# In the h stage of a chain of experts: a22 a product later, a step's sums ahead of the right sides, four later loads

## The chip, the cores and the metric

The kernel runs on one core of one Trainium2 chip. The metric is the device time of one execution, in microseconds (us). Below, PE is TensorE (its matmuls; PEld is its weight loads), DVE is VectorE, ACT is ScalarE, POOL is GpSimd, and SP is SyncE, which here only issues DMAs. SPq and ACTq are the sequencers of SP and ACT at issuing a DMA.

## The reference

The program computes an attention with 32 packed keys, a gated product of experts and a second pair of layers; the last part is what the change touches.

```python
x = attention(q, k, v, p)                 # 4608 tokens, 512 features
x = ((x @ w1) * (x @ w2)) @ w3 @ w_out    # w3 @ w_out is made first
h = x @ w_in                              # 512 -> 2048
g = where(h >= 1, h, where(h <= -1, 0, (h + 1)**2 / 4))
out = g @ w_out                           # 2048 -> 512
```

## The kernel before

Both products of the second pair of layers are made by a scheme of seven products of quarter matrices in place of eight (A11, S1, S2, A12, S4, S3, A22 are the names of the products). Every factor is kept as a high and a low part in fp32r, and a product takes three passes (high by high, high by low, low by high) over two halves of its inner dimension: six matmuls of 128x128 weights by N columns.

**The h stage** (lines 980 to 1020) has 40 steps. A step makes one 128-row piece of each quarter of h for one group of tokens; PAIRS lists five groups, each of two halves of 512 tokens (the last of 256, so N = 256 there). `divmod(s, 8)` gives the group t and the place i in it. In step s PE runs product(s, A11), product(s, S1), then product(s - 1, A22) of the step before, then S2, A12, S4 and S3 of step s. Four products of a step share one PSUM bank, "x": A11 begins it, S2, S3 and A22 add to it, and between them its value is read out. ACT copies it after A11 (m1) and after S2 (u2), and S1's bank after S1 (m5). DVE makes the sums by `add` (line 877): the first upper half from A12's bank and m1, the second from S4's bank and u2, and the first lower half from bank x after S3 and m5. A22 adds to the same bank x, so it can't begin before this last sum has read it. These sums are called the first, second and third sum of a step.

The step after applies the function g: `upper` (relu and square on ACT, two minima on DVE by line 816, a store), `upper_end` (a difference on DVE, line 843, and a store), `lower_begin`, `lower_relu`, `lower_middle` (relus and a square on ACT, two minima on DVE; the second relu and minimum read bank x after A22) and `lower_end` (a 1024-wide difference on DVE, line 866, and a store of 1 MB). The buffers U, L and r exist twice. The store DMAs are collected and issued by SP at the end of the step in program order (`flush_stores`); each waits for its data on SP, and what is behind it in SP's order waits too.

The left sides (weights of w_in, high and low) stay in memory as tiles of 1 MB: n = 0 for i = 0 to 3 and n = 1 for i = 4 to 7. All ten loads are issued by SP ahead of step 0 (lines 766 to 775). Those of S4 and A22 are streamed instead: `ws_load(s + 1)` is issued by ACT behind product(s - 1, A22), into two buffers.

The right sides of the next group (x2s tiles, high and low) are made within the steps by `x2_tasks`: a list of eleven tasks, in order parts(A11), a combination, a combination, parts(S1), a combination, parts(S2), parts(A12), parts(S4), parts(S3), a combination, parts(A22). A part is an ACT copy (line 672) and a DVE subtraction (line 673), a combination a DVE subtraction (line 667), all 1024 wide. `tasks(n)` runs the next n: MID says how many run behind the first sum of a step i, LAST how many at its end; step i = 0 has one more right behind m1's copy. The group's load (`x2_load`, 2 MB) is issued at the start of step i = 1.

**The output stage** (lines 1069 to 1093) has 140 pieces x = (group, product, quarter j) of 12 matmuls. SP loads a piece of g (`g_load`, line 930, 512 KB; two for a piece of A22, which `g_combine` on line 939 subtracts on DVE); `g_parts` makes its high part on ACT (line 947) and low part on DVE (line 948), three pieces ahead (AHEAD). In the last group of h, `first_sides` (line 957) already loads the output stage's first left sides (`w2_load`, line 907) and first pieces of g.

Of the kernel before, what the change touches and what calls it, by code (L numbers as in the profile page):

```python
# [30 lines left out]
PAIRS = [(0, 512), (1024, 512), (2048, 512), (3072, 512), (4096, 256)]  # L31

A11, S1, S2, A12, S4, S3, A22 = range(7)
# [22 lines left out]
def fused_kernel(ctx: ExitStack, tc, qT, kT, vv, pb, w1, w2, w3T, wo, win, wout, out):  # L56
# [673 lines left out]
    def buf(tag):  # L730
        if tag in first:
            return first.pop(tag)
        shape, bufs = KINDS[tag]
        return hp.tile(shape, F32, name=tag, tag=tag, bufs=bufs)
# [6 lines left out]
    def wi_load(i, n):  # L741
        nc.sync.dma_start(out=wi_t[i, n].bitcast(F32), in_=wid[i][n])
# [4 lines left out]
    def ws_load(s, eng):  # L747
        if s < 8 * len(PAIRS):
            t = ws_t[s] = first.pop("ws", None) or ws_tile()
            eng.dma_start(out=t.bitcast(F32), in_=wst[s % 8 // 4][:, s % 4])  # L750
# [20 lines left out]
    for i in (S2, A12, S3):  # L771
        wi_load(i, 0)
    ws_load(1, nc.sync)
    for i in (A11, S1, S2, A12, S3):
        wi_load(i, 1)


    BANK = {A11: "x", S1: "z", A12: "y", S2: "x", S4: "z", S3: "x", A22: "x"}
# [4 lines left out]
    def psb(b):  # L783
        return first.pop(b) if b in first else psB.tile([P, 512], F32, name=b, tag=b, bufs=BUFS[b])

    bank = {}

    def product(s, q):
        t, i = divmod(s, 8)
        N = PAIRS[t][1]  # L790
        b = BANK[q]
        if q in (A11, S1, A12):
            bank[s, b] = psb(b)
        n, c0 = divmod(i, 4)
        j = 0
        for k in range(2):
            for v, m in PASSES:
                if q in STREAM:
                    w = ws_t[s][:, STREAM.index(q), k, v, :]
                else:  # L800
                    w = wi_t[q, n][:, k, v, c0 * P:(c0 + 1) * P]
                nc.tensor.matmul(  # L802
                    bank[s, b][:, :N], w, x2_t[t, q][:, m, k, :N],
                    start=(j == 0 and q in (A11, S1, A12)), stop=(j == 5), skip_group_check=True,
                )
                j += 1
# [14 lines left out]
    def flush_stores():  # L821
        while stores:
            stores.pop(0)()

    def store(s, a, n, x):
        t, i = divmod(s, 8)
        stores.append(lambda: nc.sync.dma_start(out=gd[t][:, a:a + n, i], in_=x))
# [12 lines left out]
    def upper_end(s):  # L840
        N = PAIRS[s // 8][1]
        h = kept[s, 0]
        nc.vector.tensor_tensor(out=h[:, 2, :N], in0=h[:, 1, :N], in1=h[:, 0, :N], op=ALU.subtract)
        store(s, GT1, 1, h[:, 2:3, :N])

    def lower_begin(s):
        N = PAIRS[s // 8][1]
        r = kept[s, "r"] = buf("r")[:, :, :N]
        relu(r[:, 1], kept[s, 1][:, 1, :N])
# [21 lines left out]
    def copy(tag, ps, N):  # L871
        c = buf(tag)[:, :N]
        nc.scalar.activation(out=c, in_=ps[:, :N], func=AF.Copy)  # L873
        return c
# [7 lines left out]
    def tasks(n):  # L882
        for _ in range(n):
            if todo:
                todo.pop(0)()
# [11 lines left out]
    def half_tile(pool, tag):  # L897
        return pool.tile([P, 2, 2, 512], F32R, name=f"h{tag}", tag=tag, bufs=1).rearrange(
            "p a b (c n) -> p (a b c) n", c=2).rearrange("p (k v) n -> p k v n", v=2)

    def w2_tile(q, pool, tag):
        w = pool.tile([P, 4, 1024], F32R, name=f"w2{q}", tag=tag, bufs=1)
        w2_t[q] = [w[:, 2 * x:2 * x + 2].rearrange("p a (b n) -> p (a b) n", n=256).rearrange(
            "p (k v) n -> p k v n", v=2) for x in range(2)]

    def w2_load(q, x, k, n):
        nc.sync.dma_start(out=w2_t[q][x][:, k:k + n].bitcast(F32), in_=w2d[q][:, 4 * x + k:4 * x + k + n])
# [7 lines left out]
    def raw_tile(n):  # L915
        return buf("r") if n > 3 else ring("raw", n, [P, 2, 512], F32)
# [4 lines left out]
    def g_load(most=len(seq)):  # L921
        while count[0] < most:
            t, q, j = seq[count[0]]
            N = PAIRS[t][1]
            parts = (G21, GT2) if q == A22 else (PART[q],)
            if count[2] + len(parts) > RAWS:
                return
            for a in parts:
                g = raw_tile(count[1] % RAWS)
                nc.sync.dma_start(out=g[:, :, :N], in_=gd[t][:, a, 2 * j:2 * j + 2])  # L930
                rawg.setdefault(count[0], []).append(g[:, :, :N])
                count[1] += 1
                count[2] += 1
            count[0] += 1

    def g_combine(x):
        if x < len(seq) and seq[x][1] == A22:
            a, b = rawg[x]
            nc.vector.tensor_tensor(out=a, in0=a, in1=b, op=ALU.subtract)
# [10 lines left out]

    MID = {2: 2, 3: 1, 4: 1, 5: 1, 7: 1, 0: 2}
    LAST = {7: 2}


    def first_sides(s):
        i = s - (steps - 8)
        if i == 1:
            w2_tile(A11, late["f"], "f")  # L960
        if i in (1, 2, 3):
            w2_load(A11, (i - 1) // 2, 2 * (i - 1) % 4, 2)
        if i in (4, 5):
            w2_load(A11, 1, i - 2, 1)
        if i == 4:
            wq.release()
            late["raw"] = tc.alloc_tile_pool(name="rw", bufs=1, side="right", reuse_waits="tile")
            for n in range(4):
                tiles["raw", n] = raw_tile(n)
            w2_t[S1] = [half_tile(hp, f"wi{A11}0"), None]  # L970
        if i >= 4:
            g_load(i - 3)
        if i == 6:
            w2_load(S1, 0, 0, 2)
        if i == 7:
            w2_load(S1, 0, 2, 2)
            w2_t[S1][1] = half_tile(hp, f"wi{A11}1")
            w2_load(S1, 1, 0, 4)

    for s in range(steps):  # L980
        t, i = divmod(s, 8)
        N = PAIRS[t][1]
        if i == 1 and t + 1 < len(PAIRS):
            x2_load(t + 1)
            todo = x2_tasks(t + 1)
        product(s, A11)
        m1 = copy("m1", bank[s, "x"], N)
        if i == 0:
            tasks(1)
        if s:  # L990
            upper(s - 1)
            if i:
                upper_end(s - 1)
            lower_begin(s - 1)
        product(s, S1)
        m5 = copy("m5", bank[s, "z"], N)
        if s:
            product(s - 1, A22)
            ws_load(s + 1, nc.scalar)
        product(s, S2)  # L1000
        if s:
            lower_relu(s - 1)
        u2 = copy("u2", bank[s, "x"], N)
        if s:
            lower_middle(s - 1)
        product(s, A12)
        kept[s, 0] = buf("U")
        add(kept[s, 0][:, 0, :N], bank.pop((s, "y")), m1, N)
        if s and i:
            lower_end(s - 1)  # L1010
        tasks(MID.get(i, 0))
        kept[s, 1] = buf("L")
        product(s, S4)
        add(kept[s, 0][:, 1, :N], bank.pop((s, "z")), u2, N)
        product(s, S3)
        add(kept[s, 1][:, 1, :N], bank[s, "x"], m5, N)
        if s and i == 0:
            upper_end(s - 1)
            lower_end(s - 1)
        tasks(LAST.get(i, 0))  # L1020
        flush_stores()
        first_sides(s)
    product(steps - 1, A22)
    late["b1"].release()
# [10 lines left out]
    lower_end(steps - 1)  # L1035
    flush_stores()
    g_load()
    w2_t[S2] = [half_tile(wp, f"wi{i}0") for i in (S1, S2)]
    w2_t[A12] = [half_tile(wp, f"wi{i}1") for i in (S1, S2)]
    w2_t[S3] = [half_tile(wp, f"wi{A12}1"), half_tile(wo2, f"wi{S3}1")]  # L1040
# [3 lines left out]
    AHEAD = 3  # L1044
# [25 lines left out]
    for x, (t, q, j) in enumerate(seq):  # L1070
        N = PAIRS[t][1]
        b = BANK[q]
        start = j == 0 and q in (A11, S1, A12)
        if start:
            bank[b] = [psb(b) for _ in range(2)]
        for d in range(2):
            for k in range(2):
                for n, (s, v) in enumerate(PASSES):
                    nc.tensor.matmul(  # L1079
                        bank[b][d][:, :N], w2_t[q][j // 2][:, 2 * (j % 2) + k, s, d * P:(d + 1) * P], op[x][:, k, v, :N],  # L1080
                        start=start and k == 0 and n == 0, stop=(j == 3 and k == 1 and n == 2), skip_group_check=True,
                    )
        if x:
            flush_stores()
        if j == 3:
            evacuate(t, q, bank[b])
        if x == 0:
            g_parts(2)
        g_parts(x + AHEAD)
        g_load()  # L1090
        if t == 0 and q in order[:5]:
            w2_load(order[order.index(q) + 2], j // 2, 2 * (j % 2), 2)
        g_combine(x + AHEAD + 2)
    flush_stores()
    psB.release()
    dl.release()
# [60 lines left out]
```

## Time and profile before

| | |
|---|---|
| median of 3 runs | 1381.49 us (1380.85 to 1383.59) |
| profiled execution, its own time | 1377.88 us |
| its span | 1376.2 us |
| busy in the span: PE, PEld, DVE, ACT | 1286.0, 1066.3, 879.9, 672.1 us |
| h stage, first product to first matmul of the output stage | 617.26 to 1010.13 us |
| matmuls of the h stage (line 802), of the output stage (line 1079) | 1680, 1680 |

Times inside the trace are microseconds from the span's start. A row of the timeline gives start and duration, engine, line, operation, out<-in by the program's names, shapes and count, and in brackets how long the engine stood idle before it and what ended that. PE's busy time is not its peak, since ends of matmuls are modelled. A wait is put down to the one that came last by the profile.

### The profile page before, as it was taken

The numbers are of one execution on the slowest core, as the hardware profiler recorded it, in microseconds if no ns is written. First come the engines' busy times: TensorE is split into PE (matmuls) and PEld (weight loads), VectorE is DVE, ScalarE is ACT, GpSimd is POOL, SyncE is SP. The second block draws the span as 40 slices with busy tenths as digits, with TensorE's granted clock in tenths as the row PEclk, the third lists the DMA queues.
The fourth block names the chain that finished last, engine by engine and source line by source line (L and its number), as shares of the span: only waits on it lengthen the run. The fifth ranks groups of instructions, "written<-read, shape, count | busy, mean of one in ns | idle before, by whom it ended". The sixth has DMA issues, their size and how long they took to land.

```text
span 1376.2 us, 21142 instructions
## 1 busy us (share of the span) xinstructions
PE 1286.0 (93%) x8184; PEld 1066.3 (77%) x8184; DVE 879.9 (64%) x1462; ACT 672.1 (49%) x1144; POOL 0.7 (0%) x6
## 2 busy tenths in 40 slices
PE   6798799999999999998999989999889799999998
PEld 2365678888898989996777777778768688888888
DVE  4694387687686779534676777776664445555454
ACT  3353254545454545434576656656554243434433
POOL 0000000000000000000000000000000000000000
PEclk9899999999999999999899999999999999999999
DMA  8763366565575543359548575576899877768675
GB/s 277 240 204 112 117 225 189 187 218 179 187 243 171 209 175 134 129 177 364 186 165 298 203 257 194 176 254 223 266 385 372 317 263 234 255 229 284 221 224 173
DMA packets 124916, 306.78 MB, mean 223 GB/s; under 512 B 10384, under 2 KB 45200, under 8 KB 121360
## 3 DMA queue, kind: packets, MB, share of 16 engines
q1 hardware_dynamic: 87920, 236.09, 49.4%
q10 hardware_dynamic: 36896, 69.35, 14.9%
q8 instruction: 64, 1.05, 0.3%
q14 instruction: 36, 0.29, 0.1%
HBM read 199.36 MB, written 106.04 MB: 222 GB/s over the span
## 4 chain that ended last, share of the span: by engine, by line
PE 60%; DVE 15%; DMA 10%; ACT 9%; issue 5%; ACTq 1%; SPq 1%; DVEq 0%
PE x L1079 13%; PE psk L402 12%; PE psk L378 11%; PE z L1079 6%; PE x L802 6%; PE y L1079 4%; ACT r L810 3%; DMA g<-U 3%; PE z L802 2%; PE psk L486 2%; ACT r L813 2%; PE psk L194 2%; DMA raw<-w3T 1%; DVE L L866 1%; DVE U L877 1%
## 5 line engine op out<-in xcount | busy, mean ns | idle before, releaser
L402 PEld LDWEIGHTS psk<-g,w 128*128 128x128 f32 x1500 | 200.2, 188 | 26.3 <-ACT st L429 15.7
L378 PE MATMUL psk<-at,m 128*128 128x288 f32 x1494 | 215.2, 300 | 3.9 <-DVE at L329 1.9
L378 PEld LDWEIGHTS psk<-at,m 128*128 128x128 f32 x1494 | 202.2, 189 | 18.0 <-issue 8.6
L402 PE MATMUL psk<-g,w 128*128 128x288 f32 x1500 | 209.1, 297 | 2.6 <-ACT st L429 1.3
L802 PE MATMUL x<-x2s,wi 128*128 128x512 f32 (+1 forms) x720 | 165.9, 375 | 0.0
L802 PEld LDWEIGHTS x<-x2s,wi 128*128 128x128 f32 x720 | 129.1, 192 | 24.7
L948 DVE TENSOR_TENSOR op<-raw,op 128x1024 fp32r<-128x1024 f32 (+1 forms) x94 | 101.2, 1111 | 63.8 <-ACT op L947 63.8
L947 ACT ACTIVATE op<-raw 128x1024 fp32r<-128x1024 f32 (+1 forms) x94 | 87.1, 968 | 83.3 <-DVE L L1056 34.3
L1079 PE MATMUL x<-op,w 128*128 128x512 f32 (+1 forms) x480 | 102.7, 373 | 8.0 <-DVE op L948 8.0
L1079 PEld LDWEIGHTS x<-op,w 128*128 128x128 f32 x480 | 84.9, 191 | 25.0 <-DVE op L948 9.7
L1079 PE MATMUL x<-op,hwi 128*128 128x512 f32 (+1 forms) x480 | 100.4, 368 | 0.0
L1079 PEld LDWEIGHTS x<-op,hwi 128*128 128x128 f32 x480 | 83.1, 188 | 15.8
L802 PE MATMUL x<-x2s,ws 128*128 128x512 f32 (+1 forms) x240 | 61.0, 390 | 29.3 <-DVE L L877 29.0
L816 DVE SCALAR_TENSOR_TENSOR U<-U,r 128x512 f32<-128x512 f32 (+1 forms) x80 | 47.4, 634 | 54.5 <-ACT r L813 54.5
L390 DVE TENSOR_TENSOR tb<-psk,ta 128x288 f32<-128x288 f32 x124 | 56.1, 452 | 37.6 <-ACT ta L388 19.2
L813 ACT ACTIVATE r<-r 128x1024 f32<-128x1024 f32 (+1 forms) x80 | 78.1, 976 | 1.3
L948 DVE TENSOR_TENSOR op<-r,op 128x1024 fp32r<-128x1024 f32 (+1 forms) x46 | 50.0, 1115 | 44.4 <-ACT op L947 44.3
L486 PE MATMUL psk<-wo,w3f 128*128 128x512 f32 x128 | 64.7, 659 | 14.4 <-DVE w3f L135 14.4
L802 PEld LDWEIGHTS x<-x2s,ws 128*128 128x128 f32 x240 | 41.2, 192 | 46.3 <-DVE L L877 29.4
L873 ACT ACTIVATE m<-x 128x512 f32<-128x512 f32 (+1 forms) x40 | 22.2, 554 | 106.5 <-PE x L802 103.7
L124 ACT ACTIVATE cvt<-raw 128x512 f32<-128x512 f32 x72 | 48.3, 675 | 48.5 <-DMA raw<-w 22.7
L388 ACT ACTIVATE ta<-psk 128x288 f32<-128x288 f32 x125 | 50.4, 403 | 28.5 <-PE psk L378 24.2
(111 smaller groups left out, 1901.9 us busy)
## 6 DMA issues: line engine op xcount, KB each, us to landing
raw<-g SPq DMA_DIRECT2D x86, 512.0 KB, 4.9
g<-L SPq DMA_DIRECT2D x32, 1024.0 KB, 4.1
r<-g SPq DMA_DIRECT2D x42, 512.0 KB, 5.5
ws<-ws ACTq DMA_DIRECT2D x38, 512.0 KB, 4.5
g<-U SPq DMA_DIRECT2D x64, 256.0 KB, 4.2
w<-hl ACTq DMA_DIRECT2D x28, 512.0 KB, 3.4
x2d<-st ACTq DMA_DIRECT2D x72, 144.0 KB, 3.5
wi<-hl ACTq DMA_DIRECT2D x20, 512.0 KB, 5.4
```

Of the source, the lines that this page charges most:

```text
L124: nc.scalar.activation(out=t, in_=raw.bitcast(F32).rearrange("p (n two) -> p n two", two=2)[:, :, 1], func=AF.Copy, scale=2.0 ** -112)
L378: nc.tensor.matmul(ps[w][:, :HS], m_tile[b, w, n][:, s, G, c0 * P:(c0 + 1) * P], at_tile[b][:, G, v, hf * HS:(hf + 1) * HS], start=(k == 0 ...
L388: nc.scalar.activation(out=bs, in_=ps[1][:, :HS], func=AF.Copy)
L390: nc.vector.tensor_tensor(out=g, in0=ps[0][:, :HS], in1=bs, op=ALU.mult)
L402: nc.tensor.matmul(ps, w34[kt][:, s, mt * P:(mt + 1) * P], g_t[kt, hf][:, v, :], start=(kt == kts[0] and n == 0), stop=(kt == kts[-1] and ...
L486: nc.tensor.matmul(acc[4 * hf + m], w3f[hf, j][:, m * P:(m + 1) * P], wof[j], start=(j == 0), stop=(j == 7))
L802: nc.tensor.matmul(bank[s, b][:, :N], w, x2_t[t, q][:, m, k, :N], start=(j == 0 and q in (A11, S1, A12)), stop=(j == 5), skip_group_check= ...
L813: nc.scalar.activation(out=r, in_=r, func=AF.Square)
L816: nc.vector.scalar_tensor_tensor(out=out, in0=h, scalar=1.0, in1=r, op0=ALU.max, op1=ALU.min)
L947: nc.scalar.activation(out=o[:, :, 0, :N], in_=a[0], func=AF.Copy)
L948: nc.vector.tensor_tensor(out=o[:, :, 1, :N], in0=a[0], in1=o[:, :, 0, :N].bitcast(F32), op=ALU.subtract)
L1079: nc.tensor.matmul(bank[b][d][:, :N], w2_t[q][j // 2][:, 2 * (j % 2) + k, s, d * P:(d + 1) * P], op[x][:, k, v, :N], start=start and k == ...
```

## The change

In a step, product(s, S2) and its copy u2 now come ahead of product(s - 1, A22). The tasks that ran behind the first sum of steps i = 2 to 5 run at the end of the step, as does `lower_end` (but for i > 0 of the last group); i = 0 has one behind the first sum (parts(S3), so far right behind m1's copy) and two at the end, i = 7 stays as it was with one and two. The loads of the second halves of left sides (n = 1) are issued by SP at the end of steps 0 to 3, behind the stores of the step. One 1 MB load of the output stage's S1 moves from the end of the last step to behind the final stores and the loads of the next pieces of g. `g_combine` runs one piece later, next to that piece's `g_parts`.

```diff
     ws_load(1, nc.sync)
-    for i in (A11, S1, S2, A12, S3):
-        wi_load(i, 1)
...
-    MID = {2: 2, 3: 1, 4: 1, 5: 1, 7: 1, 0: 2}
-    LAST = {7: 2}
+    MID = {7: 1, 0: 1}
+    LAST = {2: 2, 3: 1, 4: 1, 5: 1, 7: 2, 0: 2}
...
             w2_t[S1][1] = half_tile(hp, f"wi{A11}1")
-            w2_load(S1, 1, 0, 4)
...
         m1 = copy("m1", bank[s, "x"], N)
-        if i == 0:
-            tasks(1)
...
         m5 = copy("m5", bank[s, "z"], N)
+        product(s, S2)
+        u2 = copy("u2", bank[s, "x"], N)
         if s:
             product(s - 1, A22)
             ws_load(s + 1, nc.scalar)
-        product(s, S2)
-        if s:
             lower_relu(s - 1)
-        u2 = copy("u2", bank[s, "x"], N)
-        if s:
             lower_middle(s - 1)
         product(s, A12)
         kept[s, 0] = buf("U")
         add(kept[s, 0][:, 0, :N], bank.pop((s, "y")), m1, N)
-        if s and i:
+        short = t + 1 == len(PAIRS) and i
+        if short:
             lower_end(s - 1)
         tasks(MID.get(i, 0))
...
         add(kept[s, 1][:, 1, :N], bank[s, "x"], m5, N)
-        if s and i == 0:
-            upper_end(s - 1)
+        tasks(LAST.get(i, 0))
+        if s and not short:
+            if i == 0:
+                upper_end(s - 1)
             lower_end(s - 1)
-        tasks(LAST.get(i, 0))
         flush_stores()
+        for w in {0: (A11,), 1: (S1,), 2: (S2, A12), 3: (S3,)}.get(s, ()):
+            wi_load(w, 1)
         first_sides(s)
...
     g_load()
+    w2_load(S1, 1, 0, 4)
...
-        g_combine(x + AHEAD + 2)
+        g_combine(x + AHEAD + 1)
```

## Rows read from the trace of the kernel before

**Rows 1.** The page: its first line, and a DMA issue (KB each, us to landing).
```profile
span 1376.2 us, 21142 instructions
...
g<-L SPq DMA_DIRECT2D x32, 1024.0 KB, 4.1
```
**Rows 2.** Who waited for whom, PE, the h stage.
```profile
PE x L802 <- DVE L L877: 29.0, 24, 7.1
```
**Rows 3.** Stretches cut at starts of steps: length, busy us (count), PEclk, DMA share, GB/s.
```profile
644.76:664.67 19.91, 12.76 (x43) 9.90 (x42) 10.11 (x13) 7.18 (x9) 0.00 (x0) 0.74 0.65 232
664.67:704.29 39.62, 39.05 (x169) 31.32 (x168) 27.65 (x40) 26.59 (x36) 0.00 (x0) 1.00 0.62 212
704.29:736.35 32.06, 29.66 (x127) 23.43 (x126) 25.23 (x34) 21.23 (x28) 0.00 (x0) 1.00 0.64 234
736.35:788.26 51.91, 49.19 (x211) 39.13 (x210) 37.08 (x52) 32.63 (x44) 0.00 (x0) 1.00 0.64 221
778.65:788.26 9.61, 9.61 (x43) 7.89 (x42) 6.16 (x10) 8.01 (x11) 0.00 (x0) 1.00 0.66 219
788.26:821.53 33.27, 30.97 (x128) 24.65 (x126) 25.38 (x34) 21.11 (x28) 0.00 (x0) 0.95 0.66 235
821.53:873.15 51.62, 49.20 (x212) 39.12 (x210) 36.80 (x51) 32.63 (x44) 0.00 (x0) 1.00 0.63 215
873.15:906.41 33.26, 30.97 (x128) 24.63 (x126) 25.33 (x34) 20.68 (x28) 0.00 (x0) 0.95 0.64 220
906.41:955.39 48.98, 48.46 (x211) 39.13 (x210) 34.13 (x51) 31.22 (x44) 0.00 (x0) 1.00 0.63 216
955.39:979.40 24.01, 17.65 (x127) 16.82 (x126) 16.57 (x33) 13.55 (x26) 0.00 (x0) 0.93 0.70 225
979.40:1010.13 30.73, 27.14 (x218) 25.83 (x217) 20.34 (x50) 19.68 (x43) 0.00 (x0) 1.00 1.00 328
```
**Rows 4.** Timeline of steps 15 to 17 (they start at 778.65, 788.26, 798.48).
```profile
786.09 0.69 DVE L816 SCALAR_TENSOR_TENSOR L<-x,r 128x512 f32<-128x512 f32 x1 [1.09 <-ACT r L813]
...
787.90 1.22 DVE L866 TENSOR_TENSOR L<-L,U 128x1024 f32<-128x1024 f32 x1
789.03 1.22 DVE L673 TENSOR_TENSOR x2s<-f,x2s 128x1024 fp32r<-128x1024 f32 x1
...
799.71 1.06 ACT L672 ACTIVATE x2s<-f 128x1024 fp32r<-128x1024 f32 x1 [3.09 <-DVE f L667]
...
800.67 0.58 ACT L873 ACTIVATE m<-x 128x512 f32<-128x512 f32 x1
...
803.37 2.03 PE L802 MATMUL x<-x2s,ws 128*128 128x512 f32 x6 [1.98 <-DVE L L877]
```
**Rows 5.** Timeline of steps 0 to 3, and a stretch there as in rows 3.
```profile
623.58 2.62 SPq L742 DMA_DIRECT2D wi<-wi  x5
...
649.35 0.69 DVE L877 TENSOR_TENSOR U<-y,m 128x512 f32<-128x512 f32 x1 [5.47 <-DMA g<-U]
...
637.00:647.00 10.00, 10.00 (x45) 8.23 (x44) 3.47 (x6) 5.53 (x8) 0.00 (x0) 1.00 1.01 409
```
**Rows 6.** Timeline of the last group, step 34.
```profile
975.29 0.42 DVE L877 TENSOR_TENSOR L<-x,m 128x256 f32<-128x256 f32 x1 [3.61 <-DMA g<-L]
```
**Rows 7.** Timeline of the output stage's start.
```profile
1022.69 1.06 ACT L947 ACTIVATE op<-r 128x1024 fp32r<-128x1024 f32 x1 [6.17 <-DMA r<-g]
...
1023.80 0.50 PE L1079 MATMUL z<-op,hwi 128*128 128x512 f32 x1 [2.40 <-ACT op L947]
...
1025.06 9.22 PE L1079 MATMUL z<-op,hwi 128*128 128x512 f32 x32 [0.76 <-DVE op L948]
```
**Rows 8.** Timeline of the output stage's first A22.
```profile
1077.32 1.06 ACT L947 ACTIVATE op<-raw 128x1024 fp32r<-128x1024 f32 x1 [4.31 <-DVE raw L939]
...
1084.90 1.22 DVE L939 TENSOR_TENSOR raw<-raw,raw 128x1024 f32<-128x1024 f32 x1 [6.55 <-DMA raw<-g]
...
1087.31 4.78 PE L1079 MATMUL x<-op,w 128*128 128x512 f32 x12 [5.52 <-DVE op L948]
```

## The prediction

> **What bounds the kernel now.** All the edits lie in two stages, so I read those and leave attention and the first expert layers aside. The profiled execution took 1377.88 us around a span of 1376.2 us [rows 1]; the median of the runs shown is 1381.49, 3.6 us above it. I make the sum against the profiled execution and subtract the result from the median. First view: the waits of TensorE (PE) in the h stage. It waits for almost nothing but VectorE's (DVE's) last sum of a step, 24 times, 29.0 us [rows 2]. Second view: the h stage cut at the starts of a step's first product. A step of seven products that waits for nothing takes 9.61 us, so one product takes 1.37 and a step's products begin 0, 1.37, 2.75, 4.12, 5.49, 6.86 and 8.24 us into it. Against 9.61 a step, the stretches show what waiting costs, with the slower clock after a wait [rows 3]: step 3 loses 10.3; steps 4 to 7 lose 1.2, 11 to 15 3.9, 19 to 23 3.6, 27 to 31 0.9; the steps around a new pair (8 to 10, 16 to 18, 24 to 26) lose 3.2, 4.4 and 4.4. The last pair has half the columns, 0.69 a product: steps 32 to 34 need 20 x 0.69 + 1.37 = 15.2 of their 24.0, the rest 36 x 0.69 = 24.8 of 30.7.
>
> Third view: one step's tail [rows 4]. Released by ScalarE's (ACT's) square, DVE's minima begin 7.44 into step 15 (786.09 - 778.65). Two minima and the first sum take until 9.25 (three in 1.81 us, 0.60 each), the difference of the lower half until 10.38, a right side's low part 1.13 more, and only then come the other two sums, ended by 12.7. That is 3.1 into the next step, where a22 is due at 2.75. One such part in a step's middle makes a22 about half a microsecond late; with two long operations it waits 1.98 (803.37).
>
> **The change, part by part.**
>
> *a22 a product later, sums first, in ordinary steps.* The third sum now ends 9.25 + 2 x 0.61 = 10.47 into its step, and a22 is due 9.61 + 4.12 = 13.73. That is 3.3 us of room, so a22 waits no more. The difference (1.13) and up to two long tasks (2.26) then end by 13.86, 4.25 into the next step, where DVE has nothing ready before the next square. S2 moves forward into the slot 2.75: it needs m1's copy (0.58 [rows 4]), which ACT can begin about 1.6 in (the first product and some 0.2 until its result is there, an estimate) and end at 2.2; nothing is ahead of it, since the lower square ended at 7.4 of the step before. u2's copy goes ahead of a22's relu: the same work in another order, still ended by about 7.4. The next streamed side (ws) is issued behind a22, 1.4 later, some 5.9 in, and is needed 16.5 in. I count all 1.2 + 3.9 + 3.6 + 0.9 = 9.6 of these stretches less 0.1: **-9.5** (ends -9.5 and -8).
>
> *The store of the lower half* is issued 1.2 to 3.5 us later, since its difference is now last. The buffer is written again 19.5 into the step; issued at 11.7, or 13.9 after two tasks, it has 7.8 or 5.6 us for a landing of 4.1 [rows 1]. Nothing, with 3.3 us of a22's room behind it.
>
> *A new pair (i = 7, 0, 1).* At i = 7 one part stands before the second sum and two behind the third: third sum 11.6, a22's room still 2.1. At i = 0 the part for S3 moves from just behind m1's copy to behind the first sum. ACT makes its high half early (after the square, 8.5), but DVE's low half comes after 9.25 and ends 10.4, while S3 is due 8.24. So S3 stands still about **2.05 us, a wait that was not there**. The third sum then ends 12.65, the combination 13.8, ACT's part for a22 (1.06) 14.85. m1's copy of the next step is queued behind that part and ends 15.45; S2 there is due 11.66 + 2.75 = 14.41 and waits 1.05 (the rows have such a copy, at 800.67, right behind such a part [rows 4]). a22's own low part (16.0) is in time for 16.8. So 3.1 us a boundary. The rows show what such a gap does to the clock: after a wait of 2.0 the granted clock of steps 8 to 10 is 1.00, of 16 to 18 and 24 to 26 0.95 (a part of the time at 1.2 GHz in place of 2.4), and those two take 1.2 more [rows 3, 4]. With the low clock the copy's wait is mostly absorbed: 2.05 + 1.2 = 3.25. Taking two of three again, 3.1 + 2 x 3.25 = 9.6 against 12.1: **-2.5** (-5 if the low half slips in earlier, +3 if every gap also drags the next step).
>
> *Second halves of left sides.* Before, five loads of 1 MB go out at 623.58, the next pair's 2 MB behind them, and the small stores of step 0 queue behind 7 MB: DVE's first sum waits 5.47 us for them until 649.35, while the rings move 409 GB/s [rows 5]. After, only the first load goes out there; its 1 MB and the pair's 2 MB are through by about 632, and the stores land around 635. The 10.3 of step 3 goes. The next is late instead: in SP's order the last load (S3) stands behind the lower half's store of step 3. That of step 2 goes out at 635.15 + 13.9 = 649.1, with two loads behind; then come small stores, two ws, the store of step 3 and S3's load, 6.6 MB in all, 16.1 us at 409 GB/s: 665.2. Step 4 wants S3 at 654.37 + 8.24 = 662.6: 2.6 us, and 0.7 of low clock behind the gap. **-7** (ends -9.5, the load in time, and -5).
> The Trainium skill's "DMA: Bandwidth & Descriptors" (Specifications) gives a core some 358 GB/s of HBM. By it, an estimate, the load lands 2.3 us later and this term is -4.7, the forecast 1356.6; the trace disagrees where loads lead (409 [rows 5]).
>
> *Last pair.* In step 32, S3's low part stands behind minima of the wide step before it: about 8.5 against 4.9 due, 3.6 us. Then S2 of step 33 0.9 (same queue as above), and a22 of step 34 still waits for the 1 MB store whose buffer its third sum writes (3.61 us of DVE now [rows 6]), issued no earlier: 1 to 3.5. With 1.0 for the clock, 7.8 against 24.0 - 15.2 = 8.8: **-1** (-3 to +2). Steps 35 to 39 run at a DMA share of 1.00 [rows 3]. a22's short waits go, but ws, issued 0.7 later in steps of 4.9, becomes the wait: **-1** (-2.5 to +2).
>
> *S1's 1 MB behind the first right sides of the output stage.* ACT waits 6.17 us for the fifth right side, PE 2.40 and 0.76, and 32 matmuls then take 9.22 us where 7.3 is the pace: 5.1 in all [rows 7]. Without 1 MB ahead it lands 2.6 earlier (409 GB/s), and PE waits about 0.8. The moved load lands about 1026.5 and is wanted at 1027. **-4** (-5 to 0, if the queue is simply full).
>
> *a22's sum next to its parts, output stage.* At the first a22, DVE's sum waits 6.55 us for a load until 1084.90 and holds the previous piece's low part behind it; PE stands 5.52 [rows 8]. That piece's own sum was long done: ACT made its high part at 1077.32. After, its low part follows by about 1079.6, and PE, which came to wait at 1081.8, goes on. The late load belongs to the next piece: sum until 1086.1, ACT's part 1087.2, DVE's 1088.4, against 1084.5 due, 3 to 4 us; less follows at the two pieces after it. I get **-2.2** (-9.5 if loads free up in turn, +1).
>
> Sum: -9.5 - 2.5 - 7 - 1 - 1 - 4 - 2.2 = -27.2 us; 1377.9 - 27.2 = 1350.7 for the profiled execution, and **1354.3** for the median. POOL has no part in it; SP issues the same loads.
>
> **The rivals.**
> *The loaded end gives back* (from step 35 to the first a22 the DMA rings are full, so time won is lost to the same bytes). For it: the share of 1.00. Against: PE has no wait in the middle of that stretch. Steps 32 on, the start of the output and a22 then win nothing: -27.2 + 8.2, 1362.5.
> *S3's load later still.* Loads and stores mixed at a full share moved 328 GB/s in steps 35 to 39 [rows 3]; at that rate it lands at 669.2, 4 us later: 1358.3. Against: steps 0 to 3 moved 409 with stores among the loads.
> *S2 takes a22's place.* Room of only 0.55 us behind m1's copy; if ACT is that late by another 0.4 in 39 steps, 16 us come back: 1370. Against: ACT is idle there in plain steps.
> *The waits vanish whole* at a22 in the output (7 more) and at S3's load (2.6 more): 1344.5.
> *Slower: stores of the lower half.* If each landed over 7.8 + 3.3 = 11 us after its issue, a22 would wait in all 31 wide steps; at 12.1, 1.1 us x 31 = 34 lost against 27 won: 1388. Against: 4.1 is the rule, and only a burst made it more.
> *The edit does nothing*, because the sums were not the true last wait: 1381.5. Against: the one wait of rows 2.
>
> **How the numbers follow.** Forecast 0.56, loaded end 0.14, S3's load later 0.08, S2 0.06, vanish 0.11, slower 0.03, nothing 0.02. Range 1343 to 1368: it takes in the forecast, the loaded end, the later load, the vanishing and the ends of the boundary and load terms, not all at once. A difference under 0.2%, 2.8 us, cannot be told from none here. Faster by more: 0.56 + 0.14 + 0.08 + 0.06 + 0.11 = 0.95; same 0.02; slower 0.03.
>
> **What would show it.** Right: step 3 without its 20 us; ordinary steps at 9.61; a new wait of PE before S3 at each i = 0, ended by DVE's low part, and before S2 at i = 1, ended by ACT; a wait in step 4 ended by S3's load; the fifth right side landing 2 to 3 us sooner after the stage's start. Wrong: S2 waiting in plain steps, a22 still waiting for DVE, or DVE waiting for stores of the lower half in wide steps.

## The result, and the profile after

In runs on the same chip the kernel after takes 1368.27 us (median of 12 runs, 1364.77 to 1375.99), the kernel before 1380.23 (12 runs): a ratio of 0.9914, 95% interval 0.9896 to 0.9933. It is faster, by 0.86% or some 12 us, where 27 were forecast. The profiled executions differ by 9.1 us in their own time (1377.88 to 1368.82), by 9.3 in the span, and the readings below account for those 9.3 (to 0.1).

First the page of the kernel after, which answers to [rows 1]: the span, and three kinds of transfer with their size and median time from issue to landing (before: 4.1 for the 1 MB store, 4.5 for ws, 4.2 for the small stores).

```profile
span 1366.9 us, 21137 instructions
...
g<-L SPq DMA_DIRECT2D x32, 1024.0 KB, 5.0
...
ws<-ws ACTq DMA_DIRECT2D x38, 512.0 KB, 5.8
g<-U SPq DMA_DIRECT2D x64, 256.0 KB, 6.3
```

Who waited for whom in the h stage after, PE (us in total, times, longest), and below it the same view of DVE:

```profile
PE x L800 <- ACT m L871: 7.9, 5, 2.5
PE x L800 <- DVE x2s L673: 6.2, 4, 1.6
PE x L800 <- DMA wi<-wi: 5.6, 2, 4.9
PE x L800 <- DVE L L875: 3.2, 3, 1.6
...
DVE L L875 <- DMA g<-L: 30.2, 19, 3.6
```

The 29.0 us of [rows 2] are down to 3.2, as meant. In their place stand ACT's copy m1 (ahead of S2), DVE's low part (ahead of S3) and a left side's load. DVE itself now waits 30.2 us for stores of the lower half; before it was 5.5, three times:

```profile
DVE L L877 <- DMA g<-L: 5.5, 3, 3.6
```

The stretches of [rows 3], cut at the same steps of the kernel after (step 3; 4 to 7; 8 to 10; 11 to 15; 16 to 18; 19 to 23; 24 to 26; 27 to 31; 32 to 34; 35 to 39): length, busy us (count) of PE, PEld, DVE, ACT, POOL, granted clock, DMA share, GB/s.

```profile
644.00:653.61 9.61, 9.61 (x43) 7.89 (x42) 8.48 (x12) 6.04 (x8) 0.00 (x0) 1.00 0.71 235
653.61:702.19 48.58, 42.08 (x170) 33.38 (x169) 28.33 (x40) 26.90 (x35) 0.00 (x0) 0.93 0.71 255
702.19:735.58 33.39, 29.69 (x127) 23.51 (x126) 25.05 (x33) 22.01 (x29) 0.00 (x0) 1.00 0.60 207
735.58:784.46 48.88, 48.50 (x211) 39.28 (x210) 37.14 (x51) 33.04 (x43) 0.00 (x0) 1.00 0.66 231
784.46:817.58 33.12, 29.69 (x128) 23.51 (x127) 25.08 (x33) 21.09 (x29) 0.00 (x0) 1.00 0.67 228
817.58:867.60 50.02, 48.89 (x212) 39.21 (x210) 37.15 (x51) 33.97 (x44) 0.00 (x0) 1.00 0.66 228
867.60:900.67 33.07, 29.68 (x127) 23.51 (x126) 25.51 (x34) 21.48 (x29) 0.00 (x0) 1.00 0.65 221
900.67:948.90 48.23, 48.23 (x212) 39.36 (x211) 34.15 (x51) 32.23 (x44) 0.00 (x0) 1.00 0.68 233
948.90:974.76 25.86, 20.22 (x128) 18.90 (x126) 16.96 (x33) 13.73 (x26) 0.00 (x0) 0.80 0.56 189
974.76:1007.06 32.30, 27.21 (x219) 26.01 (x217) 20.45 (x51) 20.59 (x43) 0.00 (x0) 1.00 1.00 334
```

Against 9.61 a wide step: step 3 loses nothing now (10.3 before), but steps 4 to 7 lose 10.1 (48.58 - 38.44) where they lost 1.2. That is the loss moved, not removed. Steps 11 to 15 lose 0.8, 19 to 23 2.0, 27 to 31 0.2 (3.9, 3.6 and 0.9 before): the ordinary steps got better. The new pairs lose 4.6, 4.3 and 4.2, against 3.2, 4.4 and 4.4, at a full clock. Steps 32 to 34 lose 10.7, against 8.8, and 35 to 39 7.5, against 5.9.

The table sets forecast beside measurement, in us; "losses" are such differences. Steps 4 and 5 are counted with the loads, since what they lose is a load's; the other ordinary steps are 6, 7, 11 to 15, 19 to 23 and 27 to 31.

| place | forecast | before | after | change |
|---|---|---|---|---|
| ahead of h (not touched) | 0 | | | -0.8 |
| steps 0 to 5, loss | -7 | 11.0 | 10.2 | -0.8 |
| other ordinary steps, loss | -9.5 | 8.9 | 2.9 | -6.0 |
| three new pairs, loss | -2.5 | 12.1 | 13.1 | +1.0 |
| steps 32 to 34, loss | -1 | 8.8 | 10.7 | +1.9 |
| steps 35 to 39, loss | -1 | 5.9 | 7.5 | +1.6 |
| output, first group, length | -6.2 | 91.8 | 86.6 | -5.2 |
| output, last group, length | 0 | 44.5 | 43.4 | -1.1 |
| sum | -27.2 | | | -9.4 |

**The left sides' loads.** The timeline of step 4 (it starts at 653.61), the DMA issues of SP and then PE, followed by SP's own waits there and by four stretches (columns as above).

```profile
649.33 1.56 SPq L742 DMA_DIRECT2D wi<-wi  x2
...
657.26 0.37 SPq L825 DMA_DIRECT2D g<-L  x1
659.85 0.32 SPq L742 DMA_DIRECT2D wi<-wi  x1
...
669.05 5.46 PE L800 MATMUL x<-x2s,wi 128*128 128x512 f32 x12 [4.88 <-DMA wi<-wi]
```
```profile
SPq L742 <- DMA ws<-ws: 2.2, 1, 2.2
```
```profile
636.00:649.00 13.00, 13.00 (x58) 10.69 (x57) 9.55 (x13) 10.33 (x14) 0.00 (x0) 1.00 0.75 257
649.00:669.00 20.00, 13.55 (x57) 10.18 (x55) 11.61 (x17) 9.68 (x13) 0.00 (x0) 0.98 0.97 361
...
664.00:668.00 4.00, 0.18 (x1) 0.00 (x0) 1.00 (x2) 0.00 (x0) 0.00 (x0) 1.00 1.01 410
668.00:672.00 4.00, 2.95 (x7) 2.40 (x8) 0.01 (x1) 0.00 (x0) 0.00 (x0) 0.54 0.33 128
```

S3's load is issued at 659.85, 6.2 us into the step that needs it at 8.2, and PE stands 4.88 us for it; the clock granted just after is 0.54, mostly the lower of its two levels. It goes out that late because it stands behind the lower half's store of step 3 (657.26) and because SP then waits 2.2 us more for the landing of an unrelated ws. That second wait is the program's own: in the trace the transfers tell of their landing on eight semaphores in turn, and the load's turn falls on the one of that ws. The rings had room: from 636 to 649 they moved 257 GB/s at a share of 0.75, with 3 MB of the loads not yet issued from 637 on. From 649 on everything that had been held back runs at once.

**A new pair.** The timeline around step 9 (it starts at 714.40): a minimum of step 8 on DVE, the two halts at S3 of that step, and what follows.

```profile
710.06 0.69 DVE L814 SCALAR_TENSOR_TENSOR L<-x,r 128x512 f32<-128x512 f32 x1 [0.78 <-ACT r L811]
...
711.03 0.50 PE L800 MATMUL x<-x2s,wi 128*128 128x512 f32 x1 [0.44 <-ACT x2s L672]
...
713.14 2.80 PE L800 MATMUL x<-x2s,wi 128*128 128x512 f32 x11 [1.61 <-DVE x2s L673]
...
715.52 0.69 DVE L875 TENSOR_TENSOR L<-x,m 128x512 f32<-128x512 f32 x1 [1.83 <-DMA g<-L]
...
717.38 1.06 ACT L672 ACTIVATE x2s<-f 128x1024 fp32r<-128x1024 f32 x1 [6.40 <-DVE f L667]
718.34 0.58 ACT L871 ACTIVATE m<-x 128x512 f32<-128x512 f32 x1
...
718.97 1.67 PE L800 MATMUL x<-x2s,wi 128*128 128x512 f32 x6 [1.65 <-ACT m L871]
```

The chain is the one forecast: third sum, combination, ACT's part, m1's copy queued behind it, S2. PE stands idle for S3 0.44 us until ACT's high part is there, and 1.61 us more until DVE's low part is: 2.05 in all.

**The ordinary steps** hide a new wait. The timeline of DVE in steps 12 to 14 (13 starts at 755.47), with SP's store between:

```profile
758.21 0.69 DVE L875 TENSOR_TENSOR L<-x,m 128x512 f32<-128x512 f32 x1 [1.93 <-DMA g<-L]
...
759.95 1.22 DVE L864 TENSOR_TENSOR L<-L,U 128x1024 f32<-128x1024 f32 x1
...
761.20 0.37 SPq L825 DMA_DIRECT2D g<-L  x1
...
768.47 0.69 DVE L875 TENSOR_TENSOR L<-x,m 128x512 f32<-128x512 f32 x1 [2.58 <-DMA g<-L]
```

The store leaves at 761.20, 5.7 into its step, and the next third sum goes on 7.3 us later. It is a loop: a late store makes the third sum late, that makes the next difference and its store late. Sum, one task, difference and landing take 10.26 us (758.21 to 768.47), more than a step's 9.61; in steps without a task it recovers. a22's room takes it: step 13 loses nothing.

**The last pair and the output stage.** Timeline of steps 32 and 33, then of the output stage's start and of its first A22 (answering to [rows 6 to 8]).

```profile
961.52 0.42 DVE L875 TENSOR_TENSOR L<-x,m 128x256 f32<-128x256 f32 x1 [3.57 <-DMA g<-L]
...
963.53 1.65 PE L800 MATMUL x<-x2s,wi 128*128 128x256 f32 x6 [2.51 <-ACT m L871]
...
1017.76 1.06 ACT L945 ACTIVATE op<-r 128x1024 fp32r<-128x1024 f32 x1 [4.98 <-DMA r<-g]
...
1080.05 0.50 PE L1077 MATMUL x<-op,w 128*128 128x512 f32 x1 [1.32 <-ACT op L945]
```

DVE's 3.6 us for the 1 MB store have moved from step 34 to step 32, where the combination and S2 hang on them. In the output stage the fifth right side is there 10.7 us after the stage's start (1017.76 - 1007.06), before 12.6; PE's longest single wait at the first A22 is 1.3 us, not 5.52.

### The profile page after: what moved, and what is told of

It reads as the page before. It is cut to its first block, busy times and chain, and to the rows that moved or that the text cites. A ratio compares the mean times of both kernels' runs of the same rounds, so it can differ in the third digit from the quotient of the medians.

```text
span 1366.9 us, 21137 instructions
## 1 busy us (share of the span) xinstructions
PE 1282.5 (94%) x8184; PEld 1064.5 (78%) x8184; DVE 880.9 (64%) x1462; ACT 678.3 (50%) x1144; POOL 0.7 (0%) x6
## 3 DMA queue, kind: packets, MB, share of 16 engines
q8 instruction: 64, 1.05, 0.3%
## 4 chain that ended last, share of the span: by engine, by line
PE 63%; DMA 15%; DVE 13%; ACT 6%; issue 3%; ACTq 1%; SPq 0%; DVEq 0%
PE x L1077 13%; PE psk L402 12%; PE psk L378 9%; PE x L800 8%; PE z L1077 6%; DMA g<-L 5%; PE z L800 4%; PE y L1077 4%; PE y L800 2%; DMA wi<-hl 2%; DMA raw<-w3T 2%; PE psk L194 2%; DMA ws<-ws 1%; ACT r L808 1%; PE psk L486 1%
## 5 line engine op out<-in xcount | busy, mean ns | idle before, releaser
L486 PE MATMUL psk<-wo,w3f 128*128 128x512 f32 x128 | 62.4, 639 | 14.2 <-DVE w3f L135 14.2
L945 ACT ACTIVATE op<-r 128x1024 fp32r<-128x1024 f32 (+1 forms) x46 | 43.1, 969 | 43.1 <-DVE r L937 15.1
L486 PEld LDWEIGHTS psk<-wo,w3f 128*128 128x128 f32 x128 | 25.3, 206 | 46.4 <-issue 28.4
```

The costliest lines, as they stand in the source:

```text
L486: nc.tensor.matmul(acc[4 * hf + m], w3f[hf, j][:, m * P:(m + 1) * P], wof[j], start=(j == 0), stop=(j == 7))
L945: nc.scalar.activation(out=o[:, :, 0, :N], in_=a[0], func=AF.Copy)
```

## The experiments

All are versions of the kernels before and after, timed beside the kernel before. The same view gives one table for all of them: losses of the h stage by place, length of the first group of the output, all from one profile each. The kernel "output stage alone" shares its h stage with the kernel before, and differs from it by up to some 2 us in a column: one profile of each does not tell smaller differences apart.

| kernel | ratio (interval) | 0-5 | ordinary | pairs | 32-34 | 35-39 | first group |
|---|---|---|---|---|---|---|---|
| before | | 11.0 | 8.9 | 12.1 | 8.8 | 5.9 | 91.8 |
| after | 0.9914 (0.9896-0.9933) | 10.2 | 2.9 | 13.1 | 10.7 | 7.5 | 86.6 |
| loads undone | 0.9905 (0.9885-0.9925) | 4.3 | 4.0 | 13.5 | 12.0 | 6.4 | 89.3 |
| store earlier | 0.9909 (0.9876-0.9943) | 4.8 | 3.9 | 14.0 | 11.8 | 6.0 | 88.9 |
| S3's part early | 0.9929 (0.9909-0.9949) | 9.0 | 0.0 | 20.6 | 9.7 | 6.2 | 87.3 |
| loads a step earlier | 0.9848 (0.9828-0.9868) | 0.3 | 2.7 | 13.2 | 11.0 | 6.3 | 88.8 |
| S2 ahead of a22 alone | 0.9983 (0.9960-1.0006) | 7.4 | 10.5 | 8.4 | 9.2 | 7.0 | 92.0 |
| output stage alone | 0.9964 (0.9945-0.9984) | 11.5 | 10.3 | 10.0 | 8.8 | 6.2 | 87.3 |
| tasks moved | 0.9810 (0.9779-0.9841) | 1.4 | 4.3 | 4.6 | 11.2 | 6.4 | 86.4 |
| and store earlier | 0.9795 (0.9767-0.9824) | 0.9 | 2.3 | 3.0 | 9.7 | 5.7 | 91.5 |
| combination first | 0.9769 (0.9745-0.9793) | 0.7 | 2.3 | 1.3 | 9.6 | 6.1 | 87.5 |
| sums first alone | 0.9964 (0.9948-0.9979) | 6.5 | 2.8 | 14.2 | 11.8 | 6.0 | 93.8 |

**The five second halves ahead of step 0 again**, in the kernel after.

```diff
     ws_load(1, nc.sync)
+    for i in (A11, S1, S2, A12, S3):
+        wi_load(i, 1)
...
-        for w in {0: (A11,), 1: (S1,), 2: (S2, A12), 3: (S3,)}.get(s, ()):
-            wi_load(w, 1)
```

> The changed kernel with the five second halves of left sides loaded ahead of step 0 again, the rest of the change kept. Theory (the spread of the loads only moved the stall: step 3 lost 10.3 us before, steps 4 and 5 lose 8.5 and 1.6 after): step 3 loses about 10 again, steps 4 and 5 nothing, and the time stays within 2 us of the changed kernel's 1368. Rival (the forecast's term: the spread won 7 us and something else ate it): 1375. Second rival: with a22 a product later the old burst costs less than 10, some 7, and this is 2 to 4 us faster than the changed kernel.

1365.89 us. Steps 0 to 5 lose 4.3, not 10.2: with the sums first and a22 later, the burst that cost 10.3 costs some 3 in step 3. So the spread as written gains nothing on that burst: it is worse by 5.9 us in steps 0 to 5, and by 4.1 in the h stage as a whole. The time shows less of that (the two intervals overlap), since the first group of the output is 2.7 longer in this profile.

**The lower half's end behind the first sum again**, in the kernel after.

```diff
-        short = t + 1 == len(PAIRS) and i
+        short = i > 0
```

> The changed kernel with lower_end back behind the first sum in every step but i = 0, tasks still last. Theory (in the changed kernel DVE's third sum waits 30.2 us in 19 steps for the store of the lower half whose buffer it writes, since that store is issued late and beside the streamed sides, landing in 5.5 us where it was 4.1): those waits fall below 10 us, PE's losses in steps 11, 19 and 21 (2.6 together) go, each new pair loses about 0.7 less, step 33 some 2.5 less: 1368 - 7 = 1361. Rival (a22's room hides these waits, they cost PE nothing): 1367 to 1369. Second rival (the difference ahead of the third sum makes a22 late again, as before): 1372 or more.

1366.86 us, not told apart from the kernel after. The page of this kernel has the landings of before again:

```profile
g<-L SPq DMA_DIRECT2D x32, 1024.0 KB, 4.2
...
ws<-ws ACTq DMA_DIRECT2D x38, 512.0 KB, 4.6
g<-U SPq DMA_DIRECT2D x64, 256.0 KB, 4.1
```

and DVE's waits for the store fall from 30.2 us to these:

```profile
DVE L L875 <- DMA g<-L: 6.3, 3, 3.6
```

The ordinary steps are no better for it (3.9 against 2.9): a22's room had hidden those waits. What improved is the start, 4.8 against 10.2: with the store ready sooner, S3's load leaves 1.7 us into step 4 in place of 6.2, and PE waits 2.90 for it.

**S3's part right behind m1's copy again**, in the kernel after.

```diff
-    MID = {7: 1, 0: 1}
+    MID = {7: 1}
...
         m1 = copy("m1", bank[s, "x"], N)
+        if i == 0:
+            tasks(1)
```

> The changed kernel with the part for S3 right behind m1's copy at i = 0, as before the change; nothing behind the first sum there. Theory (the wait of S3 in steps 8, 16, 24 is 2.6 us each and in step 32 3.5, made by the place of this part alone): these go, the wait of S2 in the step after stays near 1.6, and 2.6 x 3 + 3.5 = 11 us are won: 1357. Rival (DVE and ACT are full there, the part only pushes others): S2's wait in the steps after grows by as much as S3's shrinks, 1366 to 1368.

1368.54 us. The wait before S3 is gone, and the next one is larger. The timeline of step 9:

```profile
712.35 0.69 DVE L875 TENSOR_TENSOR L<-x,m 128x512 f32<-128x512 f32 x1 [3.33 <-DMA g<-L]
...
715.80 1.22 PE L800 MATMUL x<-x2s,wi 128*128 128x512 f32 x2 [5.27 <-ACT m L871]
```

PE reaches S2 sooner, but what S2 waits for begins with a third sum that stands 3.33 us for the lower half's store. Removing one end of this chain moves the wait along it.

**The loads a step earlier.**

```diff
-        for w in {0: (A11,), 1: (S1,), 2: (S2, A12), 3: (S3,)}.get(s, ()):
+        for w in {0: (A11, S1), 1: (S2, A12), 2: (S3,)}.get(s, ()):
```

> The changed kernel with the second halves of A11 and S1 at the end of step 0, of S2 and A12 at the end of step 1, of S3 at the end of step 2. Theory (the rings stood partly idle from 636 to 652, at shares of 0.57 to 0.74, because the loads came late, and S3's load then stood behind 6 MB): no wait for a load in step 4, PE's losses of 8.5 and 1.6 in steps 4 and 5 fall below 1.5 together: 1368 - 9 = 1359. Rival (the bytes are simply too many by then): a wait of 3 us or more stays somewhere in steps 2 to 4, 1365.

1358.56 us. Two stretches of this kernel, steps 1 to 7 and 632 to 648:

```profile
622.77:690.13 67.36, 67.36 (x296) 55.13 (x294) 47.16 (x66) 45.89 (x60) 0.00 (x0) 1.00 0.85 298
632.00:648.00 16.00, 16.00 (x72) 13.13 (x71) 12.55 (x17) 11.26 (x15) 0.00 (x0) 1.00 1.00 354
```

Seven steps take 67.36, 9.62 each, and the rings are full (1.00) where after had them at 0.75. The spread was right, then, and its loads a step too late; which of the four that were moved matter, besides S3's, was not tried.

**S2 and u2 ahead of a22, nothing else**, on the kernel before.

```diff
         m5 = copy("m5", bank[s, "z"], N)
+        product(s, S2)
+        u2 = copy("u2", bank[s, "x"], N)
         if s:
             product(s - 1, A22)
             ws_load(s + 1, nc.scalar)
-        product(s, S2)
...
-        u2 = copy("u2", bank[s, "x"], N)
```

> The kernel before with one edit: S2 and its copy ahead of a22. Tasks, lower_end and loads where they were. Theory (the product of room, 1.37 us, is what frees the ordinary steps; the order of DVE's sums adds little): a22's waits of 0.5 us go and those of 2.0 shrink to 0.6, ordinary steps run at 9.61, the steps around a new pair lose about 1.5 in place of 3.2 to 4.4, step 3 still loses about 8: the h stage is 14 to 18 us shorter, 1363 to 1366. Rival (the sums must come first too, since a22's wait only passes to the next step): ordinary steps still lose 0.3 or more, 1372 or above.

1376.13 us, no change that the measurement can tell. PE's waits there:

```profile
PE x L802 <- DVE L L877: 15.0, 17, 2.4
PE x L802 <- ACT m L873: 8.1, 6, 2.7
```

PE's waits for the sum fall from 24 to 17, but the ordinary steps lose as much as before (10.5): the later place alone is not it. The steps around a new pair lose less, 8.4.

**The output stage's two edits alone**, on the kernel before.

```diff
-            w2_load(S1, 1, 0, 4)
...
     g_load()
+    w2_load(S1, 1, 0, 4)
...
-        g_combine(x + AHEAD + 2)
+        g_combine(x + AHEAD + 1)
```

> The kernel before with the two edits of the output stage alone: S1's 1 MB behind the next pieces of g, a22's sum next to its parts. Theory (they work by themselves, as in the changed kernel, where the first group of the output stage takes 86.6 us in place of 91.8): about 5 us less there, the h stage as before, 1375. Rival (they only pay because h ends otherwise): the first group takes 90 us or more, 1379.

1371.48 us. The first group takes 87.3, from 91.8, with a h stage that is unchanged as a whole.

**Sums first alone**, on the kernel before: each step's sums ahead of right sides and of the lower half's end, S3's part behind the first sum, a22 where it was.

```diff
-    MID = {2: 2, 3: 1, 4: 1, 5: 1, 7: 1, 0: 2}
-    LAST = {7: 2}
+    MID = {7: 1, 0: 1}
+    LAST = {2: 2, 3: 1, 4: 1, 5: 1, 7: 2, 0: 2}
...
-        if s and i:
+        short = t + 1 == len(PAIRS) and i
+        if short:
             lower_end(s - 1)
```

> Kernel before with the order of the sums alone: each step's sums ahead of the right sides and of the lower half's end; a22 still stands behind S1's product, all loads and the output stage as before. Theory (the sums' place is what made a22 wait): the third sum ends about 0.9 us into the next step and a22 is due at 2.75, so ordinary steps lose under 0.1 each without a22's later place (before: 0.2 to 0.9), 9.6 of h's 46.7 us go, the burst at step 3 stays at 7 to 10 us and new pairs at 3 to 5 each: about 1371 us, h's excess 36 to 38. Rival: the lower half's store, now behind the sums, lands late, the upper difference that waits for its buffer delays the sums again, and a22 without a product more of room waits for them: ordinary steps lose 0.5 or more each as before, 1378 or more.

1373.28 us. The stretch of its steps 11 to 15, 1.1 over five steps of 9.61, and DVE's waits:

```profile
735.84:784.98 49.14, 48.69 (x211) 39.18 (x210) 36.81 (x51) 32.58 (x44) 0.00 (x0) 1.00 0.65 220
```
```profile
DVE L L877 <- DMA g<-L: 29.5, 18, 3.2
```

The ordinary steps lose 2.8, as after (2.9): the sums' place gives the whole gain there. DVE's waits for the store come with it too (29.5 us), and the smaller room that is left, 2 us by the forecast's own arithmetic, still nearly hides them. The theory held in the ordinary steps; the sum of losses was forecast at 36 to 38 and is 41.4, of which new pairs (14.2) and the last pair (11.8) are the excess.

**The tasks moved**, on the kernel with the loads a step earlier: S3's part at the end of i = 7, the combination behind the first sum of i = 0, A22's part at the end of i = 0.

```diff
-    LAST = {2: 2, 3: 1, 4: 1, 5: 1, 7: 2, 0: 2}
+    LAST = {2: 2, 3: 1, 4: 1, 5: 1, 7: 3, 0: 1}
```

> The changed kernel with the early loads of the run before, and at a new pair S3's part at the end of step i = 7 (three tasks there), the combination for a22 behind the first sum of i = 0 and only a22's part at its end. Theory (S3's wait comes from its part's place behind the first sum, and S2's in the step after from ACT's part for a22, which waits for a combination that waits for the third sum, which waits for a store): both waits go; steps 8 to 10, 16 to 18, 24 to 26 lose under 1.5 each in place of 4.3 to 4.7, steps 32 and 33 lose 5 or less in place of 11: 1358.6 - 14 = 1345. Rival (the stores that land late pass the wait on to whatever stands behind the third sum): the three groups still lose 3 or more each, 1355.

1350.69 us, not the 1345 expected: the pairs lose 4.6, not 13.2, some 1.5 each, about as expected, but steps 32 and 33 together 6.5 (expected: 5 or less) and step 34 4.7. **And the lower half's end behind the first sum** (`short = i > 0`) on top:

> The same with lower_end back behind the first sum in every step but i = 0. Theory (the late store is hidden by a22's room once nothing on ACT waits behind the third sum): within 2 us of the run without this edit. Rival (the late store is what costs steps 11, 15, 19 and 33): 3 to 6 us faster than it. Second rival (a third sum one difference later makes a22 late at i = 0 and in the narrow steps): 2 us or more slower.

1347.9 us; the intervals of the two overlap, so the times settle neither the theory nor its rival. The h stage loses 6.5 less in the trace, the first group of the output is 5.1 longer. **The combination right behind m1's copy** at i = 0, on top of that:

```diff
-    MID = {7: 1, 0: 1}
+    MID = {7: 1}
...
         m1 = copy("m1", bank[s, "x"], N)
+        if i == 0:
+            tasks(1)
```

> Edit to the kernel with tasks moved and the lower half's store behind the first sum (1347.9 us, stage h 21.6 us above its products' own time): at a new pair's first step the combination now runs right behind m1's copy, ahead of a22's sums, so that ACT's part is ready before S2 of step i = 1. Theory: the 1.0 us that S2 still waits in steps 9, 17 and 25, and some 1 us of step 33's 2.3, go (ACT's copy m is late only because its part of the combination is); h's excess falls to about 17.5, 1344 us. Rival 1: a22's sums, moved 0.6 us behind the combination, come late for a22 at i = 0 and give the same back there: boundaries still 1.0 each, 1347 to 1349. Rival 2: the boundaries lose nothing and the loaded last pair and output start take it back: steps 9, 17 and 25 at 0 but 1347 to 1348.

1345.05 us, 2.3% under the kernel before, the lowest of all. PE's waits for m1's copy in the h stage, 4.5 us in five places in the version before it, are one:

```profile
PE x L800 <- ACT m L871: 1.0, 1, 1.0
```

Steps 9, 17 and 25 lose 0.0, as the theory has it; steps 10, 18 and 26 now lose 0.4, 0.7 and 0.2 at a22, and step 34 loses what 33 gained. So the wait that was aimed at went, but the h stage gained 1.5 us, not 4, and the times of the two versions overlap.

## Why the prediction was wrong

The sign was right, and so were the gain in the ordinary steps, the places of the waits at a new pair, and the output stage. The size was not, and four terms of the sum made the difference.

**Second halves of left sides (-7, came out at -0.8).** This is the step that failed most. The forecast had S3's load land at 665.2, from 6.6 MB at 409 GB/s. It had landed by 669.05, and PE waited 4.88, not 2.6. The issues were much as forecast: the two loads of step 2 left at 649.33 (forecast 649.1), and S3's stood behind the store of step 3, as the forecast said. Three things were not: SP's wait for an older transfer's landing, 2.2 us, was left out; 7.2 MB had moved by then, not 6.6; and the rate from 649 to 669 was 361 GB/s on average, over half of it stores and streamed sides. It was 410 only at the end (664 to 668). The rival "S3's load later still" has the time nearly right (669.2), by luck in part: it took 328 GB/s throughout. What each of the three cost was not separated. The Trainium skill's "DMA: Bandwidth & Descriptors" (Specifications) puts a core's share of HBM at some 358 GB/s. The 361 lie near it but average slower and faster stretches, and the 409 of [rows 5] and the 410 here lie above it, so the trace does not bear it out as a limit.

The smaller waits before S2 and A12 (0.77 and 0.85) were not in the sum at all. The low clock was in it at 0.7 and cost more: steps 4 and 5 lose 10.1, of which the three waits are 6.5; the other 3.6 fall where the granted clock is 0.54 and 0.60 (668 to 672 and 672 to 676). And step 3's 10.3 was not the loads' alone: with the old loads and the new order it is some 3, so two terms of the sum claimed the same microseconds. Shown by the two experiments on the loads.

**A new pair (-2.5, came out at +1.0).** Both waits came at their places. That S3's idle time is the 2.05 of the forecast is luck in part: the forecast's own 10.4 - 8.24 is 2.16, and 0.44 of the idle time is for ACT's high part, which it took to be early. Such a halt costs its step 2.6: DVE's minima begin 7.87 into step 8 (710.06 - 702.19), not 7.44, with u2's copy and the issue of ws now ahead of ACT's last relu, and so the low part ends 10.9 in, not 10.4 (S3's first matmul runs alone before that). S2's wait was 1.3 to 1.65 and cost 1.6 to 2.0, not 1.05, the third sum ahead of it having waited 1.83 for a store; and no low clock absorbed it: the granted clock of these stretches is 1.00. So 4.2 to 4.6 a boundary, not 3.1 to 3.25. That the tasks' places make these losses is shown by two runs: S3's part put early alone makes the chain behind it worse (20.6), S3's part and the combination both put earlier take 13.2 down to 4.6. The combination was not moved alone in the kernel after. Sums first alone has 14.2 and S2 ahead of a22 alone 8.4, so the rise goes with the sums' order and the tasks that moved with it, as far as one profile of each can tell.

**The store of the lower half (nothing).** The landing was taken as 4.1; in these steps it is 7.3 where the rows above show it, and the page has 5.0. The store now leaves in the same two microseconds as ws and the small stores, and DVE waits 30.2 us for it. As a price on PE in ordinary steps "nothing" was nearly right, by the room named for it. It was wrong where there is no room: the third sum in front of the combination at i = 0, step 32, and step 11 (below). The slower rival, the same mechanism at 1388, needed 11 us for a landing.

**The last pair (-1 and -1, came out at +1.9 and +1.6).** The forecast left the 3.6 us wait for the 1 MB store in step 34, with ends up to +2; it came in step 32, where a combination, a part and S2 hang on it, and S2 of step 33 stood 2.51, not 0.9. No version took these three steps under 8.8; their clock is 0.80 to 0.93, and what bounds them was not isolated. In steps 35 to 39 the forecast had a22's waits go and ws take their place. PE's waits in that stretch after:

```profile
PE x L800 <- DVE L L875: 2.8, 2, 1.6
PE z L800 <- DMA ws<-ws: 2.1, 2, 1.2
```

The same two rows of before have 2.4 and 1.0. So ws became later as forecast, by 1.1 us of waits, but a22's waits stayed: with the rings at 1.00 the sum that a22 waits for comes no sooner. Neither was tried alone.

**The ordinary steps (-9.5, came out at -6.0).** Right in kind; the gain is the sums' place, not a22's. The forecast credited both together; sums first alone reaches 2.8, S2 ahead of a22 alone 10.5. What is left is 1.7 in step 19 and 0.7 in step 11. In step 19 DVE's first sum waits 2.95 for the small stores, in flight beside the 2 MB load of the next pair, m1's copy stands behind it and S2 behind that; that the load delays them was not tried. In step 11 a22 waits for a third sum that stands for the lower half's store:

```profile
739.50 0.69 DVE L875 TENSOR_TENSOR L<-x,m 128x512 f32<-128x512 f32 x1 [2.46 <-DMA g<-L]
```

**The output stage (-4 and -2.2, came out at -5.2).** Right: the fifth right side came 1.9 sooner, and the first A22's late low part no longer holds the piece before it. The last group's 1.1 us were overlooked. They come with the two edits (43.4 or 43.5 us in every version with them, 44.5 to 45.1 without); why is not shown, since the three groups between have an A22 each too and stay at 76.6. The rival "the loaded end gives back" was right that steps 32 to 39 would win nothing, but the output's gain stayed, and most of the missing 15 us lies ahead of step 32. In the better versions the first group varies from 86.4 to 91.5 with no edit there, so some of each later gain does come and go at this end; why was not settled.

## What to carry to other kernels

When work is moved off a hot engine's path, follow the transfers that leave with it: here the sums' order gave the gain of the ordinary steps, and loads that were issued later cost 10.2 us in steps 0 to 5, which fell to 0.3 when they left a step earlier. Spread a burst of loads by when each is needed less its queue, not by one per step, and look at whether the rings are full while a load waits to be issued. Where a chain of small steps (sum, combination, part, copy) ends at the critical engine, moving one link only moves the wait; move the links together.

## What was not expected of the hardware

Landing times depended on what left together more than on how much: with the same bytes per step and a DMA share of 0.62 to 0.71 in ordinary steps before and after, the medians of the 1 MB store, ws and the small stores went from 4.1, 4.5 and 4.2 us to 5.0, 5.8 and 6.3, and back to 4.2, 4.6 and 4.1 when the store alone left some microseconds earlier. A load on SP's queue stood 2.2 us for the landing of a transfer of another queue with which it shares no data, only a semaphore; the trace of before has such waits in larger (SP's loads of g behind out's stores, 11.4 us at the longest).
